# Weights in 1 KB runs, a permuted channel order, a split last unit and a new hand-written order in a two-attention kernel

## The chip, the cores and the metric

The kernel runs on one core of a Trainium2 chip. The metric is the device time of one execution in microseconds. PE is the matmul engine, PEld its weight loads, DVE, ACT and POOL are the three elementwise engines, and SP is the engine that does little but issue DMA transfers. ACT can issue them too.

## The reference

Two attentions follow each other. The second is a layer of four attention experts, of which each row takes the two with the largest gate logits.

```python
# 1: B, H, S, D = 4, 8, 768, 64; n_global, n_local = 8, 96
scores = q @ k.T / sqrt(D) - slope[h] * dist          # dist: row - column, or n_local for a far global key
keep = (column < n_global) | (0 <= row - column < n_local)
x = softmax(where(keep, scores, -1e9)) @ v            # then (B, S, H*D) with H*D = 512 channels

# 2: E = 4 experts, Hd = 64, the two best of four per row
logits = x @ w_gate
for e in range(E):
    ye = causal_softmax((x @ wq[e]) @ (x @ wk[e]).T / sqrt(Hd)) @ (x @ wv[e]) @ wo[e]
    out += weight_of(e, top2(logits)) * ye            # softmax over the two best logits
```

## The kernel before, in words

The rows are cut into 24 units of 128 rows (4 batches of 6; u counts them). Every unit goes through the same stages, and the string `ORDER` says by hand in which order the stages of all units are put into the program: a slot is a stage's two letters, the unit and, where there is a choice, the engine (`a` ACT, `g` POOL, `v` DVE, `s` SP). Each engine works through its own part of that list strictly in order.

- `lk lq lv` load a unit's keys, queries or values (256 KB, in runs of 256 bytes) into one of six buffers for each of the three, on SP's queue or on ACT's (L238). `wi` loads the weights of an expert projection (512 KB; 0 is wk, 1 wq, 2 wv, 3 wo, and 4 the small gate), `wc` turns them into 16 bits.
- `kc qc vc vx` cast keys, queries and the two parts of values to 16 bits (L258, L267). `tk tq` transpose keys and queries on PE, and one copy (L285) brings both to `kqT`.
- `sa sb` make the local scores of a unit, in two halves: first a matmul with the bias table `biasT` (L345), then keys times queries (L352), then one exponential on ACT (L355). `gs vg` do the same for the eight global keys.
- `va vb` multiply scores and values (L381) in one PSUM buffer of two banks, `zps`. DVE takes the reciprocal of the sums (L388) and multiplies (L390), which gives `x`. `tx` transposes x (L402, L403).
- `pk pq pv` project x to the experts' keys, queries and values (L414, L428); `ro` takes a step of the routing (L533 to L557).
- `ca cb cc` make causal scores (L459) and exponentials (L462), `ma` zeroes what lies above the diagonal (L474).
- `za zb` multiply scores and values of the experts (L487) in the same PSUM buffer; DVE normalizes and weighs them after `zb` (L494 to L498), which gives `zs`. `tz` transposes it (L509, L512), `ou` multiplies by wo (L519), copies (L522) and stores (L523).
- `wm` puts in matmuls on the identity that nobody reads, while PE waits at the start (L248).
- `xb` makes the bias table, `xm xc xk xs xi` other constants. `ck` checks that all row sums were in range (L741, L742); their count decides at the very end whether a slow general path has to follow. With these inputs it doesn't.

PSUM has three pools: `psS` with two buffers of two banks (scores), `psZ` with one of two banks (both attentions' values), and `psT` with two buffers of one bank (transposes, projections, outputs).

The projections sum over the 512 channels of x in four groups of 128 (`ko`). Which channels form a group doesn't matter, as long as x and the weights agree. The loads of the weights are written so:

```python
issue(w32s[i][:, :, :, :],
      (moe_wk, moe_wq, moe_wv)[i].rearrange("e (ko kp) d -> kp e ko d", kp=P))
```

Group ko is here made of the channels from 128*ko on, and a partition's row of a weight is four runs of 64 numbers for each expert.

Of the kernel before, what the change touches and what calls it, by code (L numbers as in the profile page):

```python
# [18 lines left out]
P = 128  # L19
# [3 lines left out]
def kernel(  # L23
# [59 lines left out]

    def bias_constants(_):
        V.tensor_copy(rel[:, :], rel_i[:, :])
        ge = const.tile([P, W], F32, name="ge")
        V.tensor_scalar(ge[:, :], rel[:, :], 0.0, None, op0=Alu.is_ge)
        lt = const.tile([P, W], F32, name="lt")
        V.scalar_tensor_tensor(lt[:, :], rel[:, :], float(NL), ge[:, :],
                               op0=Alu.is_lt, op1=Alu.mult)  # L90
        V.tensor_scalar(lt[:, :], lt[:, :], -1.0, -NEG, op0=Alu.add, op1=Alu.mult)
        V.tensor_scalar(rel[KB:P, :], rel[KB:P, :], slopes[1] / slopes[0], None, op0=Alu.mult)
        for p in range(NP):
            V.scalar_tensor_tensor(biasT[:, p, :], rel[:, :], -slopes[2 * p] / sc1, lt[:, :],
                                   op0=Alu.mult, op1=Alu.add)
# [57 lines left out]
    def weights_in(i, on):  # L153

        issue = queues[on]
        if i == 4:
            w32s[i] = wst.tile([P, NK, E], F32, name="wg32", tag="wg32", bufs=1)
            issue(w32s[i][:, :, :], moe_w_gate.rearrange("(ko kp) e -> kp ko e", kp=P))
            return
        w32s[i] = wst.tile([P, E, NK, Hd], F32, name="w32", tag="w32")  # L160
        if i < 3:
            issue(w32s[i][:, :, :, :],
                  (moe_wk, moe_wq, moe_wv)[i].rearrange("e (ko kp) d -> kp e ko d", kp=P))
        else:
            issue(w32s[i][:, :, :, :].rearrange("p e k d -> p (e k d)")
                  .rearrange("p (a m) -> p a m", a=NEP),
                  moe_wo.rearrange("(a b) d m -> (b d) a m", b=2))
# [31 lines left out]
    NC, current = 120, {}  # L199
# [33 lines left out]
    s16s, zs_, x16s, routing, zss, zts, tps, ppss, zs2 = ({} for _ in range(9))  # L233
# [7 lines left out]
    def keep_warm(n):  # L241
# [5 lines left out]
        for _ in range(n):  # L247
            mm(current["z"][:, 0, 4 * P - 2 * NC:4 * P].rearrange("r (a n) -> r a n", a=2),  # L248
               lhsT=ident[:, :], rhs=ident[:, 0:NC].unsqueeze(1).to_broadcast([P, 2, NC]),
# [110 lines left out]
    def global_values(u):  # L360
# [3 lines left out]
        for hf in range(2):  # L364
            r = slice(hf * Dh, hf * Dh + Dh)
            mm(zs_[u][:, hf, 0:HG * VW].rearrange("r (h d) -> r h d", h=HG),  # L366
# [3 lines left out]
    def local_values(u, i):  # L370
# [4 lines left out]
        for hq in (2 * i, 2 * i + 1):  # L375
            for prev in range(2 if ri else 1):
                for c in range(2):
                    for hf in range(2):
                        r = slice(hf * KB, hf * KB + KB)
                        at = c * (2 * P - KB) + prev * P  # L380
                        mm(zs_[u][:, hf, hq * VW:(hq + 1) * VW],  # L381
# [3 lines left out]
        if i == 1:  # L385
            z4 = zs_[u][:, :, 0:HG * VW].rearrange("r a (h d) -> r a h d", h=HG)
            rinv = rinv1[:, b, ri, :].rearrange("r (a h) -> r a h", a=2)
            V.reciprocal(rinv, z4[:, :, :, Dh])  # L388
            x16s[u] = pp.tile([P, 2, HG, Dh], F16, name="x16", bufs=5)
            V.tensor_tensor(x16s[u][:, :, :, :], z4[:, :, :, 0:Dh],  # L390
                            rinv.unsqueeze(3).to_broadcast([P, 2, HG, Dh]), op=Alu.mult)

    def turn_x(u, on):

        xTs[u] = pp.tile([P, NK, P], F16, name="xT", bufs=4)
        x16 = x16s[u][:, :, :, :].rearrange("r a h d -> r (a h d)")
# [80 lines left out]
    def causal_values(u, i):  # L477
# [6 lines left out]
        z_ps = zs2[u][:, 0, 0:E * VW].rearrange("r (e d) -> r e d", e=E)  # L484
        for e in range(i * E // 2, (i + 1) * E // 2):
            for ci in range(n):
                mm(z_ps[:, e, :], lhsT=a2[:, e % 2, (e // 2) * n + ci, :],  # L487
                   rhs=held("v2buf", b * NT + ci)[:, e, :], start=(e == 0 and ci == 0), stop=True,
                   skip_group_check=True)
        if i == 0:  # L490
            return
        assert next(routing[u // NH], "end") == "end"
        rinv = rinv2[:, b, ri, :]
        V.reciprocal(rinv, z_ps[:, :, Hd])  # L494
        ce = pp.tile([P, E], F32, name="ce")
        V.tensor_mul(ce[:, :], rinv, wts[u // NH][:, ri % NH, :])
        zss[u] = pp.tile([P, E, Hd], F16, name="zs")
        V.tensor_tensor(zss[u][:, :, :], z_ps[:, :, 0:Hd],  # L498
                        ce[:, :].unsqueeze(2).to_broadcast([P, E, Hd]), op=Alu.mult)

    def turn_z(u, on):
        zts[u] = pp.tile([P, NEP, P], F16, name="zt")
        if on == "s":
            nc.sync.dma_start_transpose(zts[u][:, :, :],
                                        zss[u][:, :, :].rearrange("r e d -> r (e d)"))
            return
        zt_ps = psT.tile([P, NEP, P], F16, name="ztps", tag="t")
# [6 lines left out]
    def output(u, on):  # L514
        b, ri = divmod(u, NT)
        assert 3 in ready
        o_ps = psT.tile([P, D], F32, name="ops", tag="t")
# [5 lines left out]
        dma(out[b, ri * P:(ri + 1) * P, :], o_sb[:, :])  # L523

# [34 lines left out]
    def general_path(ctx):  # L559
# [35 lines left out]

        ident32 = gc.tile([P, P], F32, name="ident32")
# [20 lines left out]
        with tc.For_i(0, B, 1) as b:  # L617
# [43 lines left out]
            for ri in range(NT):  # L661
                l_ps = gp.tile([P, MAXB], F32, name="gs", tag="s", bufs=2)
                for ko in range(NK):
                    mm(l_ps[:, 0:E], lhsT=xT[:, ko, ri * P:(ri + 1) * P],
                       rhs=wvg16[:, ko, E * Hd:E * Hd + E],
# [6 lines left out]
            for e in range(E):  # L672
                for w, dst, nm in ((wq16, qs, "q"), (wk16, ks, "k")):
                    d = gb.tile([Hd, S], F16, name=f"g{nm}T{e}")
                    for c in range(2):
                        p_ps = gp.tile([P, MAXB], F32, name="gs", tag="s", bufs=2)
                        for ko in range(NK):
                            mm(p_ps[0:Hd, 0:S // 2], lhsT=w[:, ko, e // 2, e % 2, :],
# [6 lines left out]
                for ct in range(NT):  # L685
                    p_ps = gp.tile([P, MAXB], F32, name="gs", tag="s", bufs=2)
                    for ko in range(NK):
                        mm(p_ps[:, 0:Hd], lhsT=xT[:, ko, ct * P:(ct + 1) * P],
                           rhs=wvg16[:, ko, e * Hd:(e + 1) * Hd],
# [55 lines left out]
    def branch_hint(_):  # L745
# [8 lines left out]
        "vs": (select_values,), "xb": (bias_constants,), "xi": (half_identities,),  # L754
# [9 lines left out]
    }  # L764
    for slot in ORDER.split():
        stage, *args = stages[slot[:2]]
        if slot[-1].isalpha():
# [7 lines left out]
    n_f = const.tile([1, 1], F32)  # L775
    V.reduce_sum(n_f[:, :], n_ps[:, :], axis=Ax.X)
    n_i = const.tile([1, 1], I32)
    V.tensor_copy(n_i[:, :], n_f[:, :])
# [13 lines left out]
xb0 lk0s kc0v lq0s az0v az1g lk1s xi0a xs0v xk0g lq1a wm14 tk0 qc0g lv0s kc1g lk2s lq2s lk3a  # L792
wm5 tq0a lq3s xc0g lv1a lv2s lq4s lk4a qc1v lq5s vc0g vx0g wm4 tk1 tq1v xm0v lk5s wm10 sa0 sb0
wm10 vs0 gi0 wi0a wm2 gs0 lk6s kc2v qc2v tk2 tq2v wm3 gs1 lq6s wm7 vg0 kc3g va0 vb0 vc1g vx1v
qc3a sa1 az2g sb1 tk3 tq3v tx0v wi1a vg1 az3g qc4a vc2g kc4g vx2v wm2 va1 wm4 sa2 sb2 vb1 qc5g
gs2 kc5a wc0g tk4 tq4v tx1v az4v lv3s vg2 va2 lv4s vb2 sa3 sb3 tk5 tq5v wm6 tx2v kc6a lq7s wi2a
qc6v wm4 sa4 sa5 tk6 vc3g tq6v pk0 sb4 sb5 wc1v pk1 wm2 gs3 wm2 pq0a vx3v pq1a gi1 vg3 vc4g
vx4g wi4s lv5s va3 vb3 lk7a ca0 ma0 pk2 pq2v tx3v ca1 vg4 va4 vb4 lq8s ca2 pk3 pq3a lk8s vc5v
vx5v cb2 vg5 wc2g lv6s kc7g lq9s pv0v pv1v lq10a lk9s qc7g qc8g kc8g ca3 cb3 tk7 lv7s tq7v pv2v
ro0 va5 sa6 tk8 tq8v tx4v vc6g vx6g lk10a lk11s vb5 sb6 gs4 lv8s ro0 pv3v pk4 qc9g pq4v ro0 ro0  # L800
lq11s lq12a ma1 vs1 lk12s lk13a sa7 tx5v kc9g pv4v kc10g ma2 vg6 va6 ro0 vb6 ca4 tk9 tq9v pk5
lk14s lq13s lv9a pq5v cb4 tx6v sb7 vc7v qc10g qc11a vx7g vc8g tk10 tq10v pv5v kc11g kc12g lq14a
qc12g cc4 vg7 va7 lq15s vb7 ro0 ro0 pk6 pq6a tk11 tq11v vx8g sa8 sb8 tx7v lk15s kc13g kc14g za0
qc13g zb0 lv10a tk12 tq12v gi2 pv6a sa9 sa10 ro1 ro1 lv11s lv12s vc9v vg8 va8 vb8 pk7 pq7a vx9g
tk13 tq13v lk16s lk17s gs5 ca5 qc14g lq16s tz0v za1 lq17s ro1 tk14 tq14v zb1 tx8a ro1 sb9 vc10g
vx10g sb10 kc15a pv7v pv8v vc11g vg9 va9 kc16a vb9 sa11 sa12 tz1v ro1 lq18s kc17v pk8 pq8a za2
ro1 tk15 zb2 sb11 sb12 qc15g tq15v tx9a vc12g vx11g vg10 va10 lk18s vx12g qc16g qc17v vb10 gs6
vs2 tk16 tq16v wi3s qc18g kc18g tk17 tq17v ma3 cb5 vg11 ma4 lk19s va11 lv13s lv14s cc5 tx10v
lv15s tk18 tq18v vb11 ca6 pv9v pv10a ro1 sa13 ro2 sa14 lq19s lq20s gi3 lq21s wc3g za3 ro2 zb3
ou0v ou1a vc13g ro2 ca7 lq22s ca8 vx13g vg12 ma5 va12 vb12 tx11v pk9 pq9v za4 ro2 lk20s kc19g  # L810
zb4 lk21s lk22s lv16s ma6 tz2a ro2 sb13 sa15 tx12v qc19v qc20g pk10 pq10a vc14g vx14g kc20g ma7
tz3v vg13 vc15g ro2 va13 vb13 lv17a cb8 gs7 ma8 ou2v tk19 tq19v lk23s lv18a za5 sb14 sb15 tz4v
zb5 tx13a pv11v sa16 ro2 sb16 vg14 va14 vb14 pk11 ro3 lv19s lv20a pq11a pv12v sa17 za6 zb6 ro3
ro3 vc16g vx15g vx16g ou3a ou4v qc21v ca9 lv21s cb9 tk20 kc21g tq20v za7 pk12 zb7 pq12a tx14v
vc17g ca10 vx17g ro3 cb10 vg15 va15 qc22g tz5v tz6v vb15 ou5a vc18g vc19g tk21 tq21v sa18 vc20v
sb17 kc22g kc23g za8 zb8 tx15a pk13 pq13v ca11 vg16 cc10 va16 pv13v lv22a pv14v cb11 ma9 vb16
gs8 ou6a pk14 pq14v ca12 vx18g vg17 va17 vb17 ca13 tz7v ro3 pk15 ro3 ro3 vx19v pq15a sb18 vs3
tx16v tx17v za9 zb9 ro4 pk16 lq23s pq16a ou7v ro4 lv23s qc23g cc11 vg18 va18 vc21g vb18 pv15a
tk22 tq22v sa19 sa20 ma10 pv16v ma11 za10 tz8a zb10 sb19 sb20 ro4 ro4 ro4 pv17v tz9v ca14 vg19
va19 vb19 ou8a ou9a vx20v sa21 sb21 ro4 ro4 tk23 tq23v ro5 za11 tx18v zb11 tz10a sa22 sb22  # L820
tx19v ma12 pv18v cb14 vg20 va20 vb20 gs9 ro5 ou10a pv19v ma13 vx21g ca15 ca16 vc22g za12 tz11v
zb12 pk17 pq17v pk18 pq18v ro5 ma14 ro5 vc23g cb15 vx22g vg21 va21 vb21 cb16 ro5 tx20v ro5 ro5
pk19 pq19a za13 zb13 pv20a ro6 sa23 sb23 tx21v vg22 va22 vb22 cc16 tz12v pk20 ro6 pq20a za14
# [47 lines left out]
```

## Time and profile before

| | |
|---|---|
| median of 3 runs | 153.25 us (151.09 to 156.71) |
| the profiled execution | 152.97 us |
| its span in the profile | 150.8 us, so 2.2 us lie around it |
| busy share | PE 93%, PEld 73%, DVE 74%, ACT 72%, POOL 60% |
| moved by DMA | 27.77 MB, 85364 packets, of which 82000 under 512 bytes |

The span is what the trace covers, from the first instruction to the last. Busy shares are means over stages that differ: the inputs arrive during the first 87 us, and the last batches are worked off after that. A PE that is shown busy need not be at its peak, since matmuls overlap; the number of matmuls in a stretch says more. The chain that ended last is 74% PE and 11% DMA.

### The profile page before, as it was taken

The numbers are of one execution on the slowest core, as the hardware profiler recorded it, in microseconds if no ns is written. First come the engines' busy times: TensorE is split into PE (matmuls) and PEld (weight loads), VectorE is DVE, ScalarE is ACT, GpSimd is POOL, SyncE is SP. The second block draws the span as 40 slices with busy tenths as digits, with TensorE's granted clock in tenths as the row PEclk, the third lists the DMA queues.
The fourth block names the chain that finished last, engine by engine and source line by source line (L and its number), as shares of the span: only waits on it lengthen the run. The fifth ranks groups of instructions, "written<-read, shape, count | busy, mean of one in ns | idle before, by whom it ended". The sixth has DMA issues, their size and how long they took to land.

```text
span 150.8 us, 7217 instructions
## 1 busy us (share of the span) xinstructions
PE 140.3 (93%) x3029; PEld 110.2 (73%) x3029; DVE 111.4 (74%) x348; ACT 108.1 (72%) x176; POOL 90.2 (60%) x254
## 2 busy tenths in 40 slices
PE   5799999999999999999978999999999999999760
PEld 4567778887778888878757778888778878786520
DVE  4838676687899887878863987687787777778850
ACT  4027657778576888888638998887977978989640
POOL 7278351568878988797827899136286345463200
PEclk9999999999999999999999999999999999999999
DMA  4999998999999989899899963415221005013462
GB/s 99 280 252 286 276 261 192 254 247 238 277 282 275 245 201 249 189 256 208 231 240 288 301 166 113 116 43 142 74 77 70 4 19 195 24 51 127 155 263 97
DMA packets 85364, 27.77 MB, mean 184 GB/s; under 512 B 82000, under 2 KB 82000, under 8 KB 85328
## 3 DMA queue, kind: packets, MB, share of 16 engines
q1 hardware_dynamic: 62496, 21.51, 56.6%
q10 hardware_dynamic: 22832, 5.77, 17.1%
q8 instruction: 24, 0.39, 1.0%
q14 instruction: 12, 0.10, 0.2%
HBM read 20.98 MB, written 6.29 MB: 181 GB/s over the span
## 4 chain that ended last, share of the span: by engine, by line
PE 74%; DMA 11%; DVE 4%; POOL 3%; ACT 2%; issue 1%; SPq 1%; ACTq 0%; POOLq 0%; DVEq 0%
PE pps L414 14%; PE cps L459 7%; PE vps L428 7%; PE tp L283 7%; PE ops L519 6%; PE zps L487 6%; PE zps L381 6%; PE sps L345 5%; PE zps L248 4%; DMA kf<-in_k_dram 4%; DMA vf<-in_v_dram 4%; PE xps L402 3%; PE sps L352 3%; DMA qf<-in_q_dram 3%; PE zps L366 2%; PE ztps L509 2%
## 5 line engine op out<-in xcount | busy, mean ns | idle before, releaser
L462 ACT ACTIVATE a<-cps 128x1024 f16<-128x1024 f32 (+1 forms) x48 | 42.2, 917 | 8.3 <-PE cps L459 6.6
L355 ACT ACTIVATE abuf<-sps 128x636 f16<-128x636 f32 (+1 forms) x48 | 30.6, 686 | 12.8 <-PE sps L352 10.1
L267 POOL CAST vbuf<-vf 64x256 f16<-64x256 f32 x76 | 31.0, 408 | 8.4 <-DMA vf<-in_v_dram 5.2
L474 POOL TENSOR_SCALAR_AFFINE_SELECT a<-a 128x256 f16<-128x256 f16 x48 | 18.3, 409 | 5.1 <-ACT a L462 4.8
L285 DVE COPY kqT<-tp 128x1024 f16<-128x1024 f16 x23 | 15.7, 688 | 6.6 <-PE tp L283 6.1
L390 DVE TENSOR_TENSOR x<-zps,rinv 128x512 f16<-128x512 f32 x24 | 16.6, 691 | 0.8
L487 PE MATMUL zps<-v2buf,a 128*128 128x65 f16 x336 | 16.0, 193 | 0.6 <-DVE zs L498 0.5
L345 PE MATMUL sps<-biasT,ident 64*64 64x318 f16 (+1 forms) x192 | 14.5, 305 | 1.4 <-ACT abuf L355 1.3
L381 PE MATMUL zps<-vbuf,abuf 64*128 64x65 f16 x704 | 15.5, 189 | 0.0
L258 POOL CAST s16k<-kf 128x512 f16<-128x512 f32 x17 | 10.3, 612 | 8.7 <-DMA kf<-in_k_dram 8.3
L487 PEld LDWEIGHTS <-a 128*128 128x128 f16 x336 | 13.3, 97 | 2.1 <-DVE zs L498 0.9
L381 PEld LDWEIGHTS <-abuf 64*128 64x128 f16 x704 | 14.0, 94 | 1.1 <-issue 0.2
L414 PE MATMUL pps<-xT,wk 128*128 128x128 f16 x192 | 14.7, 219 | 0.0
L414 PE MATMUL pps<-xT,wq 128*128 128x128 f16 x192 | 14.5, 219 | 0.0
L248 PE MATMUL zps<-ident 128*128 128x240 f16 x75 | 12.8, 316 | 1.7 <-POOL ident masks.py:199 1.6
L428 PE MATMUL vps<-wvg,xT 128*128 128x260 f16 x96 | 13.9, 275 | 0.0
L459 PEld LDWEIGHTS <-kq 64*128 64x128 f16 x336 | 9.7, 94 | 5.8 <-issue 4.4
L459 PE MATMUL cps<-kq,kq 64*128 64x128 f16 x240 | 13.8, 218 | 0.0
L519 PE MATMUL ops<-wo,zt 128*128 128x512 f16 x48 | 13.5, 380 | 0.4 <-DVE zt L512 0.4
L352 PE MATMUL sps<-kqT 64*64 64x159 f16 (+2 forms) x384 | 13.8, 223 | 0.0
L258 POOL CAST s16q<-qf 128x512 f16<-128x512 f32 x15 | 9.4, 630 | 5.1 <-DMA qf<-in_q_dram 4.9
L414 PEld LDWEIGHTS <-wk 128*128 128x128 f16 x192 | 11.5, 98 | 0.8
(113 smaller groups left out, 286.4 us busy)
## 6 DMA issues: line engine op xcount, KB each, us to landing
out_dram<-osb SPq DMA_DIRECT2D x24, 256.0 KB, 2.3
qf<-in_q_dram SPq DMA_DIRECT2D x20, 256.0 KB, 5.6
kf<-in_k_dram SPq DMA_DIRECT2D x19, 256.0 KB, 5.7
vf<-in_v_dram SPq DMA_DIRECT2D x17, 256.0 KB, 5.5
vf<-in_v_dram ACTq DMA_DIRECT2D x7, 256.0 KB, 4.7
kf<-in_k_dram ACTq DMA_DIRECT2D x5, 256.0 KB, 4.9
qf<-in_q_dram ACTq DMA_DIRECT2D x4, 256.0 KB, 4.5
w<-in_moe_wk_dram ACTq DMA_DIRECT2D x1, 512.0 KB, 5.3
```

Source lines behind the costliest of these rows:

```text
L248: mm(current["z"][:, 0, 4 * P - 2 * NC:4 * P].rearrange("r (a n) -> r a n", a=2), lhsT=ident[:, :], rhs=ident[:, 0:NC].unsqueeze(1).to_bro ...
L258: copies[on](s16s[nm, u][:, :, :], fs[nm, u][:, :, :])
L267: copies[on](o[hf * KB:(hf + 1) * KB, c, :, 0:Dh], fs["v", u][c * KB:(c + 1) * KB, hf * HG:(hf + 1) * HG, :])
L345: mm(s_ps[o, hh, 0:2 * w].rearrange("r (c n) -> r c n", c=2), lhsT=ident2[r, :], rhs=biasT[r, p, 0:w].unsqueeze(1).to_broadcast([KB, 2, w] ...
L355: S_.activation(as_[u][:, :, g, :].rearrange("r h (c n) -> r h c n", c=2)[:, :, :, 0:w], s_ps[:, :, 0:2 * w].rearrange("r h (c n) -> r h c ...
L381: mm(zs_[u][:, hf, hq * VW:(hq + 1) * VW], lhsT=as_[u - prev][r, hq % 2, hq // 2, at:at + P], rhs=held("vbuf", u - prev)[r, c, hq, :], sta ...
L414: mm(p_ps[:, i, ep, :], lhsT=w[:, ko, ep, :, :].rearrange("r a d -> r (a d)"), rhs=xT[:, ko, :], start=(i == 0 and ep == 0 and ko == 0), s ...
L428: mm(v_ps[:, :], lhsT=xT[:, ko, :], rhs=wvg16[:, ko, :], start=(ko == 0), stop=(ko == NK - 1))
L459: mm(s_ps[:, e2, i, :], lhsT=kqs[b * NT + ci][r, 0, ep, :], rhs=kqs[u][r, 1, ep, :], start=(i == 0), stop=True, skip_group_check=True)
L462: S_.activation(a2[:, :, 4 * c:4 * c + len(part), :], s_ps[:, :, 0:len(part), :], func=Exp, scale=sc2)
L487: mm(z_ps[:, e, :], lhsT=a2[:, e % 2, (e // 2) * n + ci, :], rhs=held("v2buf", b * NT + ci)[:, e, :], start=(e == 0 and ci == 0), stop=Tru ...
L519: mm(o_ps[:, :], lhsT=zts[u][:, ep, :], rhs=wo16[:, ep, :], start=(ep == 0), stop=(ep == NEP - 1))
```

## The change

1. The weights wk, wq and wv come in runs of 1 KB: a partition gets four neighbouring channels of an expert (256 numbers). So group ko is now made of every fourth channel, and x is written in that order. The heads stand 128 apart in PSUM instead of 65, so that one access pattern covers all eight. The matmuls that keep PE busy write to the free columns between them.
2. The constants for the bias table are made in two slots, `xb` and `xp`. The masks `xm`, `xc` and the half identities `xi` are made on POOL.
3. The last unit is normalized, transposed and multiplied by wo in halves: experts 0 and 1, then 2 and 3, each half in its own bank. Its output is copied in two halves by DVE and ACT and stored over both queues. Outputs of units 21 and 22 and the transpose of 22 use `psS` instead of `psT`.
4. At the end the sum of the checks is written as a whole number at once.
5. `ORDER` is new throughout. It starts with query tile 0, and 60 matmuls of `wm` are left of 75. ACT issues 7 loads instead of 19. The general path loads its own weights in the old order.

```diff
-            issue(w32s[i][:, :, :, :],
-                  (moe_wk, moe_wq, moe_wv)[i].rearrange("e (ko kp) d -> kp e ko d", kp=P))
+            issue(w32s[i][:, :, :, :].rearrange("p e k d -> p e (k d)"),
+                  (moe_wk, moe_wq, moe_wv)[i].rearrange("e (kp ko) d -> kp e (ko d)", ko=NK))
...
-    NC, current = 120, {}
+    NC, current = 60, {}
...
-                        mm(zs_[u][:, hf, hq * VW:(hq + 1) * VW],
+                        mm(zs_[u][:, hf, hq * P:hq * P + VW],
...
-            x16s[u] = pp.tile([P, 2, HG, Dh], F16, name="x16", bufs=5)
-            V.tensor_tensor(x16s[u][:, :, :, :], z4[:, :, :, 0:Dh],
-                            rinv.unsqueeze(3).to_broadcast([P, 2, HG, Dh]), op=Alu.mult)
+            x16s[u] = pp.tile([P, NK, H, Dh // NK], F16, name="x16", bufs=5)
+            V.tensor_tensor(x16s[u][:, :, :, :].rearrange("r k h d -> r h k d"),
+                            z8[:, :, 0:Dh].rearrange("r h (d k) -> r h k d", k=NK),
+                            rinv.unsqueeze(2).unsqueeze(3).to_broadcast([P, H, NK, Dh // NK]),
+                            op=Alu.mult)
...
+        last = u == NU - 1
+        nz = E // 2 if last else E
...
-        if i == 0:
+        if i == 0 and not last:
             return
...
+    def end_tile(u, first, shape, dtype, name):
+        if u < first:
+            return psT.tile(shape, dtype, name=name, tag="t")
+        return psS.tile(shape, dtype, name=name, tag="s")
...
+    def last_output(ep):
+        b, ri = divmod(NU - 1, NT)
+        if ep == 0:
+            outs["last"] = [psS.tile([P, 2, D], F32, name="ops1", tag="s")] * 2
+        for i in range(2):
+            c = slice(i * D // 2, (i + 1) * D // 2)
+            o_ps = outs["last"][i][:, i, 0:D // 2]
+            mm(o_ps, lhsT=zts[ep, "last"][:, :], rhs=wo16[:, ep, c], start=(ep == 0),
+               stop=(ep == NEP - 1), skip_group_check=True)
+        if ep == 0:
+            return
+        for i, (copy, queue) in enumerate(((V.tensor_copy, dma), (S_.copy, S_.dma_start))):
+            c = slice(i * D // 2, (i + 1) * D // 2)
+            o_sb = pp.tile([P, D // 2], F32, name=f"osb{i}", bufs=1)
+            copy(o_sb[:, :], outs["last"][i][:, i, 0:D // 2])
+            queue(out[b, ri * P:(ri + 1) * P, c], o_sb[:, :])
...
-xb0 lk0s kc0v lq0s az0v az1g lk1s xi0a xs0v xk0g lq1a wm14 tk0 qc0g lv0s kc1g lk2s lq2s lk3a
+bh0 lq0s xm0g xk0g lk0s lk1a xc0g xb0 lq1s lv0s xp0 xi0g lk2s lk3s xs0g qc0v kc0a qc1v kc1a
+wm18 tk0 lq2a az0v lq3a wm7 tk1 kc2g tq0v wm2 tq1a wm13 sa0 wm2 tk2 lk4s gi0 az1g az2g vc0v
...
-ck0 ck1 ca23 bh0 cb23 za21 tz19v zb21 ou18v cc23 tz20v ma22 za22 zb22 tz21a ou19a ou20v ma23 za23 tz22v
-zb23 ou21a ou22a tz23v ou23a ck2
+cb23 ou17v tz19a za21 zb21 cc23 ck0 ck1 ma22 ou18v za22 tz20v zb22 ma23 tz21a ou19a ou20a za23
+tz22a zb23 ou21a ou22a tz23v ty23v ck2 ou23 oy23
```

## The prediction

> **What bounds the kernel now.** I read the page first, then a table of stages, then the waits of the worst stage with the chain that runs through it, then the timeline of the end. The page:
>
> ```profile
> span 150.8 us, 7217 instructions
> ...
> PE 140.3 (93%) x3029; PEld 110.2 (73%) x3029; DVE 111.4 (74%) x348; ACT 108.1 (72%) x176; POOL 90.2 (60%) x254
> ...
> DMA  4999998999999989899899963415221005013462
> ```
>
> The DMA row is full until slice 23 (87 us): inputs flow that long. Stages (columns: stretch, its length, busy us and count of each engine):
>
> ```profile
> 0.00:25.00 25.00, 21.73 (x342) 16.31 (x346) 16.95 (x50) 11.71 (x21) 13.48 (x46) 1.00 1.08 240
> 25.00:75.00 50.00, 50.00 (x1202) 40.63 (x1195) 40.61 (x116) 38.68 (x64) 39.74 (x99) 1.00 1.06 240
> 75.00:80.00 5.00, 3.62 (x79) 2.90 (x78) 2.96 (x9) 2.38 (x5) 1.32 (x4) 1.00 1.06 240
> 80.00:135.00 55.00, 54.95 (x1273) 44.48 (x1272) 41.65 (x137) 46.80 (x75) 32.95 (x98) 1.00 0.39 111
> 135.00:140.00 5.00, 4.93 (x84) 3.00 (x79) 4.47 (x19) 4.80 (x7) 1.96 (x8) 1.00 0.33 121
> 140.00:147.00 7.00, 5.07 (x64) 2.83 (x63) 4.77 (x21) 3.75 (x7) 0.77 (x2) 1.00 0.53 204
> ```
>
> PE sets the pace: 24 matmuls/us from 25 to 75 us, 23 from 80 to 135. It loses time in three places: the start, 75 to 80 us (16/us: 79 matmuls are 3.3 us of work, so 1.7 us lost), and the end. The waits from 60 to 80 us and the chain there name the middle loss:
>
> ```profile
> POOL s16k L258 <- DMA kf<-in_k_dram: 3.8, 2, 3.5
> ACT abuf L355 <- PE vps L428: 2.3, 1, 2.3
> ...
> PE sps L345 <- ACT abuf L355: 1.3, 1, 1.3
> ```
>
> and in the chain, with start and length in us:
>
> ```profile
> 73.47 4.66 DMA qf<-in_q_dram
> ...
> 78.20 0.39 ACTq L238
> ```
>
> ACT was not waiting for PE: its sequencer stood before a load of v (slot `lv18a`) that could not be issued until an earlier q load had landed at 78.13, and the exponential behind it started 2.3 us late. The end:
>
> ```profile
> 143.75 1.02 PE L519 MATMUL ops<-wo,zt 128*128 128x512 f16 x4
> ...
> 144.22 0.42 DVE L498 TENSOR_TENSOR zs<-zps,ce 128x256 f16<-128x256 f32 x1
> ...
> 145.02 0.27 PE L509 MATMUL ztps<-ident,zs 128*128 128x128 f16 x2 [0.24 <-ACT osb L522]
> ...
> 145.33 0.29 DVE L512 COPY zt<-ztps 128x256 f16<-128x256 f16 x1 [0.68 <-PE ztps L509]
> ...
> 145.68 0.60 PE L519 MATMUL ops<-wo,zt 128*128 128x512 f16 x2 [0.39 <-DVE zt L512]
> ...
> 146.32 0.59 ACT L522 COPY osb<-ops 128x512 f32<-128x512 f32 x1 [0.86 <-PE ops L519]
> ```
>
> Last scores times values done at 143.75; then a single file of steps, PE nearly idle, to 146.91; the store and the closing waits take 3.9 us more.
>
> **What the Trainium skill says.** "DMA: Bandwidth & Descriptors", Why small descriptors are slow: each packet has a fixed cost, 27% of a 256-byte one. The trace agrees in direction. ACT's ring moved 22832 packets, 5.77 MB, in 17.1% of 16 engines' span: 0.171 x 150.8 x 16 / 22832 = 18 ns per 256 bytes. SP's ring (62496 packets, 56.6%) holds 3328 of 2 KB; the other 59168 at 18 ns leave 89 ns for each of those, 45 ns per KB instead of 72. Same page, Anatomy of one DMA: the engines that move data don't wait on semaphores, the issuing sequencer does. That is the 2.3 us above. "VectorE: DVE Perf Modes", Mode 1x: the base mode makes no assumptions on strides or PSUM operands. No run of before shows a strided read of this size.
>
> **The change, part by part** (against the profiled execution: 152.97 us, span 150.8; the median shown is 153.25).
>
> 1. *Weights in 1 KB runs.* Three loads of 512 KB: 6144 packets x 18 ns become 1536 x 45 to 72 ns. Saved: 0 to 42 us of engine time, over 16 engines 0 to 2.6 us of supply, all before 35 us. I take 1.2; it pays only where supply binds, so it is joined to part 4.
> 2. *Every fourth channel side by side.* The order of channels on both sides of the projections is the same permutation; matmul shapes and counts stay (heads at a pitch of 128 in the two PSUM banks instead of 65). The multiply that writes x reads PSUM 4 words apart and writes runs of 16. Before: 691 ns for 512 elements, and 424 for 256, so 1.04 ns an element, one per cycle. At that rate a stride has nothing to spoil: I take 0; below zero there is no reason; above, half rate is 24 x 0.53 us, kept for a rival.
> 3. *First loads, bias constants in two parts, masks moved to POOL.* Before, the first scores start at 11.03, behind key tile 1, third on SP's ring (landed just before POOL's cast at 8.05). Now key tile 1 has ACT's first slot, and query tile 1 takes the third place on SP: cast by 8.5, transposed by 8.85, then ACT's copy (1.01, as kqT by ACT before) under 13 warm-ups (1.3 us): scores at 10.2. DVE has 0.27+1.10+0.32+0.24+0.26 of constants, 4 small ones of 0.15 and 1.03 of biases first, about 5.9, then the query casts: not late. So 0.8 us earlier. But the stage after it is fed by DMA at an unchanged rate: counting slots, k12's cast has 41 tile volumes ahead in both orders, and as much PE work done. I take 0; bounds -0.8 and +0.3. Fifteen warm-ups fewer (75 to 60, 0.1 us each) stood in waiting time: 0.
> 4. *The new order, middle.* Loads on ACT's queue go from 19 to 7, and after the first 30 us only one (`lq23a`) is left. The 1.7 us that PE lost go, about 12 x 0.4 us of issuing leave ACT, and SP has them instead; they use the same engines. The first outputs now stand behind lk22 instead of ahead of lk20. What is late next: v14's cast (65 tile volumes ahead, one less through part 1), which POOL takes in order ahead of v13's second half and a mask. Before, the count of landed volumes ran at 1.04 us each up to 53 and 1.10 up to 66. At 1.05 v14 lands at 71, about when PE comes there; at 1.10 at 74, 3 us late. With part 1, I take -2.0; bounds -3.5 and +1.5. Casts and copies by engine come out even: by the row durations DVE 59.7 to 59.0 us, ACT 29.0 to 30.1, POOL 55.3 to 54.5.
> 5. *The checks of row sums* (`ck0 ck1`, 1.0 us of DVE at 138.9) stood ahead of unit 21's normalization, and unit 22's matmuls waited 0.7 us for it (PEld L487, from 140.26). They now come after it: -0.6; bounds -0.8 and 0.
> 6. *Last unit in halves.* T = 143.75. Half 0's normalization runs under half 1's 12 matmuls (0.36) and the outputs of 21 and 22 (4 x 0.217). Half 1: 0.17 + 0.16 + (0.157 + 128 x 1.04 ns = 0.29) and gaps: T+0.76. PE is free at T+0.87 and no longer waits for ACT's copy (other PSUM pool); two transposes and their latency T+1.15, two small copies (0.2 each, half of the 0.286 row and a fixed part) T+1.5, four matmuls of 256 columns, the last two after it, T+1.85; copies of 256 columns on DVE (0.43, as v2buf's cast) and ACT (0.37) together T+2.3. Before: T+3.16. So -0.85, with the store unchanged (2.3 us to landing; two halves on two rings can save 0.1). `ck2` (0.43 of DVE) lies under the four matmuls. I take -0.9; bounds -1.2 and -0.5. One conversion fewer at the very end (0.14) is under the store.
>
> Sum: -2.0 -0.6 -0.9 = -3.5: 149.4 us (span 147.3).
>
> **Rivals.**
> - *Supply takes the place of ACT's wait.* PE reaches v13's and v14's values early and waits behind POOL's cast. For: POOL's waits above, 3.5 us for one key tile; two thirds of the former ACT loads now stand in SP's single file. Against: SP's own order puts no output ahead of them. The -2.0 becomes 0 to +0.5: 151.5 to 152. 0.27.
> - *The strided multiply runs at half rate.* x takes 1.2 us instead of 0.69, between the one PSUM buffer of attention and the projections, 24 times. For: never seen here. Against: one element per cycle already. It decides from about 1.0 us up; if 60% of 12.7 us reaches PE's path: 149.4 + 7.6 = 157, slower. 0.09, with a somewhat smaller share for a milder form, 154.
> - *A denser plan than the sum shows.* The whole order is new; if the start's 0.8 us keeps and PE runs at 24 a us throughout (1273 + 84 + 64 matmuls after 80 us: 59 us instead of 67, of which a quarter is got): 149.4 - 0.8 - 2 = 146.6. 0.16.
> - *The new order is worse in places that I can't see*: 153.5. 0.06.
>
> **How the numbers follow.** Forecast 0.42: 149.4, own range 147.8 to 151. Range 146.3 to 152.9, which takes in the denser plan's value and the supply rival. A measurement of this kernel tells about 2% from no change; 2% below 153 is 150.0. Faster: the denser plan and nearly four fifths of the forecast, 0.16 + 0.33 = 0.49. Slower: the strided multiply and part of the worse order, 0.13. The rest, 0.38, same.
>
> **What would show it.** Right: no idle of 1 us or more on ACT ahead of an exponential from 70 to 80 us; the gap of PE there gone; x at 0.69 us; the last store issued about 2.3 us after the last scores times values; the first scores before 10.5 us. Wrong: POOL waiting for v14 with PE idle at 70 to 78 us; x above 0.8 us; fewer than 23 matmuls per us after 80 us.

## The result, and the profile after

The changed kernel is slower: 172.91 us median (171.84 to 174.87), beside 153.39 us for the kernel before in the same runs. The ratio is 1.134 (95% interval 1.112 to 1.156), where the prediction had 149.4 us; ratios, here and below, leave out executions in which the core ran disturbed. Its profiled execution took 171.84 us with a span of 170.0. The page of the kernel after, with the rows of total busy time, DMA share, rate and DMA queues:

```profile
span 170.0 us, 7194 instructions
...
PE 140.9 (83%) x3016; PEld 110.7 (65%) x3016; DVE 109.8 (65%) x335; ACT 109.7 (64%) x181; POOL 93.5 (55%) x266
...
DMA  5999899999896999988979949013210413322450
GB/s 116 218 218 221 177 313 239 196 212 224 176 226 146 230 200 213 224 185 185 254 168 212 260 140 227 13 64 125 83 48 4 129 66 125 125 94 99 185 197 2
...
q1 hardware_dynamic: 73952, 25.57, 64.9%
q10 hardware_dynamic: 6528, 1.71, 5.2%
```

And the rate row of the kernel before:

```profile
GB/s 99 280 252 286 276 261 192 254 247 238 277 282 275 245 201 249 189 256 208 231 240 288 301 166 113 116 43 142 74 77 70 4 19 195 24 51 127 155 263 97
```

PE's busy time is unchanged (140.9 against 140.3 us, at a granted clock of 0.97 against 1.00); all of the 19 us is waiting. The DMA row is as full of nines as before, and that is what misled: a full row says that the engines had packets in hand, not how fast these went. The rate row says it: in the first slices that carry nothing but loads, 218, 218, 221 GB/s in place of 280, 252, 286. The same 16 engines, no more bytes, and about a fifth slower. The stages of the kernel after:

```profile
0.00:25.00 25.00, 19.09 (x325) 14.21 (x329) 14.73 (x42) 11.11 (x18) 14.78 (x52) 0.95 1.07 209
25.00:75.00 50.00, 41.09 (x961) 33.17 (x954) 31.41 (x83) 31.03 (x54) 31.61 (x78) 0.99 0.99 206
75.00:80.00 5.00, 2.58 (x72) 1.97 (x69) 2.76 (x7) 3.73 (x6) 0.95 (x2) 1.00 0.87 190
80.00:135.00 55.00, 52.63 (x1187) 42.73 (x1191) 40.07 (x126) 40.83 (x67) 35.40 (x103) 0.97 0.55 135
135.00:140.00 5.00, 5.00 (x135) 3.95 (x124) 3.60 (x13) 4.68 (x8) 3.77 (x13) 1.00 0.24 74
140.00:163.00 23.00, 20.40 (x366) 14.66 (x364) 17.06 (x66) 18.00 (x30) 7.02 (x23) 1.00 0.33 126
```

From 25 to 75 us the last column falls from 240 to 206 GB/s and PE's matmuls from 1202 to 961. The waits of the kernel after from 70 to 81 us, where the prediction looked for ACT's wait and its successor:

```profile
POOL s16k L264 <- DMA kf<-in_k_dram: 4.7, 2, 3.7
...
PE tp L289 <- POOL s16k L264: 3.2, 1, 3.2
```

ACT's wait is gone; a key tile is late instead, POOL waits for it and PE for POOL. Three single lines answer other steps: the multiply with the strided read of PSUM, the first local scores, and the last store of ACT's half:

```profile
L397 DVE TENSOR_TENSOR x<-zps,rinv 128x512 f16<-128x512 f32 x24 | 16.6, 691 | 0.8
...
10.74 0.33 PE L351 MATMUL sps<-biasT,ident 64*64 64x318 f16 x4
...
163.30 0.37 ACTq L566 DMA_DIRECT2D out_dram<-osb  x1
```

**What slows the loads** is, as the experiments show, two things that the diff hardly shows. First, the change drops a constant of four bytes, `n_f` (the count was first summed as a float and then turned into a whole number; now it is summed as one). It was the last tile but one of the pool of constants and took 32 bytes of every partition. All buffers that are allocated later lie 32 bytes lower in the built program: the input buffers begin at 78304 in place of 78336. 78336 is 306 times 256; 78304 is 32 bytes short of that. The buffers are 2 KB each and follow each other, so every run of 256 bytes that a load of keys, queries or values writes now lies across a multiple of 256. Second, the new order leaves ACT 7 loads of 19: 73952 of the packets are now in one ring (q1) and 6528 in the other (q10), against 62496 and 22832.

### The profile page after: what moved, and what is told of

It reads as the page before. It is cut to its first block, busy times and chain, and to the rows that moved or that the text cites. A ratio compares the mean times of both kernels' runs of the same rounds, so it can differ in the third digit from the quotient of the medians.

```text
span 170.0 us, 7194 instructions
## 1 busy us (share of the span) xinstructions
PE 140.9 (83%) x3016; PEld 110.7 (65%) x3016; DVE 109.8 (65%) x335; ACT 109.7 (64%) x181; POOL 93.5 (55%) x266
## 3 DMA queue, kind: packets, MB, share of 16 engines
q1 hardware_dynamic: 73952, 25.57, 64.9%
q10 hardware_dynamic: 6528, 1.71, 5.2%
## 4 chain that ended last, share of the span: by engine, by line
PE 40%; DMA 26%; SPq 14%; POOL 7%; DVE 4%; issue 2%; ACT 2%; POOLq 0%; DVEq 0%
SPq L244 13%; DMA kf<-in_k_dram 13%; PE pps L423 6%; DMA qf<-in_q_dram 6%; PE ops L534 5%; PE cps L468 5%; PE zps L498 5%; DMA vf<-in_v_dram 4%; PE vps L437 4%; DMA w<-in_moe_wk_dram 3%; PE zps L387 3%; PE tp L289 2%; PE sps L351 2%; PE xps L411 2%; PE ztps L524 2%
## 5 line engine op out<-in xcount | busy, mean ns | idle before, releaser
L273 POOL CAST vbuf<-vf 64x256 f16<-64x256 f32 x74 | 29.8, 403 | 8.0 <-DMA vf<-in_v_dram 4.9
L264 POOL CAST s16k<-kf 128x512 f16<-128x512 f32 x15 | 9.2, 611 | 19.8 <-DMA kf<-in_k_dram 18.3
L289 PE MATMUL tp<-ident,s16k 128*128 128x128 f16 x96 | 9.6, 224 | 9.7 <-POOL s16k L264 6.2
L423 PE MATMUL pps<-xT,wq 128*128 128x128 f16 x192 | 15.1, 223 | 0.2 <-POOL wq L180 0.2
L498 PEld LDWEIGHTS <-a 128*128 128x128 f16 x336 | 13.4, 98 | 2.5 <-DVE zs L511 1.1
L428 ACT CAST kq<-pps 128x512 f16<-128x512 f32 x13 | 7.5, 586 | 10.3 <-PE pps L423 10.1
L289 PEld LDWEIGHTS <-s16k 128*128 128x128 f16 x96 | 6.0, 99 | 12.2 <-POOL s16k L264 6.9
L468 PE MATMUL cps<-kq,kq 64*128 64x128 f16 x240 | 13.1, 218 | 0.3 <-DVE kq L428 0.3
L264 POOL CAST s16q<-qf 128x512 f16<-128x512 f32 x17 | 10.3, 611 | 5.1 <-DMA qf<-in_q_dram 4.5
```

Source lines behind the costliest of these rows:

```text
L264: copies[on](s16s[nm, u][:, :, :], fs[nm, u][:, :, :])
L273: copies[on](o[hf * KB:(hf + 1) * KB, c, :, 0:Dh], fs["v", u][c * KB:(c + 1) * KB, hf * HG:(hf + 1) * HG, :])
L289: nc.tensor.transpose(tps[u][:, i, p, :], s16[:, p * P:(p + 1) * P], ident[:, :])
L423: mm(p_ps[:, i, ep, :], lhsT=w[:, ko, ep, :, :].rearrange("r a d -> r (a d)"), rhs=xT[:, ko, :], start=(i == 0 and ep == 0 and ko == 0), s ...
L468: mm(s_ps[:, e2, i, :], lhsT=kqs[b * NT + ci][r, 0, ep, :], rhs=kqs[u][r, 1, ep, :], start=(i == 0), stop=True, skip_group_check=True)
L498: mm(z4[:, e // nz, e % nz, :], lhsT=a2[:, e % 2, (e // 2) * n + ci, :], rhs=held("v2buf", b * NT + ci)[:, e, :], start=(e % nz == 0 and c ...
```

## The experiments

Ratios are to the kernel before, run beside each; the interval is 95%.

**One ring, in the kernel before** (`e1_before_one_ring`): all 19 loads of ACT are put on SP's queue, each at its place in the order.

```diff
-lk0s kc0v lq0s ... xk0g lq1a wm14 ... lq2s lk3a
+lk0s kc0v lq0s ... xk0g lq1s wm14 ... lq2s lk3s
```

> The kernel before with one thing changed: all its loads are issued by SP, at the same places of the order (19 of them were ACT's). Theory A (one issuer's ring alone moves inputs more slowly than two together: 1.1 us against 0.91 us for a 256 KB tile in the two traces): the inputs end some 10 us later, 160 to 167 us, tile landings 1.05 to 1.15 us apart, under 230 GB/s. Theory B (rings don't matter, loads on ACT only hold ACT up): 150 to 153 us, ACT's 2.3 us idle at 76 us is gone. Theory C (the new order asks for tiles in a worse sequence; queues don't matter): 152 to 154 us.

1.086 (1.078 to 1.095). The kernel before, its code and buffers untouched, loses 8.6% when SP issues everything. My theory that a load on ACT's queue only costs ACT time falls with this run: with the second ring the inputs come faster.

**Two rings, in the kernel after** (`e2_after_two_rings`): every third tile load on ACT, 25 in all.

> The changed kernel with one thing changed: every third tile load goes to ACT's queue, at its place in the order (25 tile loads on ACT instead of 6; the weights stay on SP). Theory A: landings back at 0.9 to 1.0 us per tile up to 80 us, 156 to 164 us. Theory B: more loads on ACT hold it up more, 174 to 178 us. Theory C (sequence of tiles): 171 to 174 us.

1.134 (1.126 to 1.142): nothing comes back. So the one ring can't be all.

**The changed code with the old order** (`e3_after_code_old_order`), and the same with the loads of v17 and v18 on SP and the first two checks behind unit 21's normalization (`e4_mix`; the expectation counts v16 too, which SP issued already):

```diff
-zb23 ou21a ou22a tz23v ou23a ck2
+zb23 ou21a ou22a tz23v ty23v ck2 ou23 oy23
```

> The code of the changed kernel (1 KB weight runs, permuted channels, split last unit, late outputs in the scores' PSUM pool) with the order of the kernel before, its queues too; only the last slots and the second half of the bias constants are adapted. If order and queues alone made it slow (A or C): 150.5 to 153 us, the tail 0.9 us shorter. If the code did (strided multiply, weights in 1 KB runs): 160 us or more.

> As the one with the new code and the old order, with the loads of v16, v17 and v18 issued by SP instead of ACT, and the first two checks of row sums put behind unit 21's normalization. Theory A: these loads come late, when the inputs are nearly all in, so one ring costs little and ACT's 1.3 and 2.3 us before them go: 1 to 2.5 us less than the old order with the new code, 148 to 151 us. If the waits on ACT were only covering a later limit (v landing on POOL): no difference.

1.071 (1.068 to 1.074) and 1.067 (1.059 to 1.075). With 19 loads on ACT and the order of before (e3), the new code alone is 7% slower, although none of its instructions takes longer. Its first loads, issued at the same times as before's, landed later from the first ones on (the third at 6.68 us, not 6.20; the sixth at 10.31, not 8.89). That pointed away from order and waits, to where the bytes go.

**Only the address, in the kernel before** (`e8_before_shifted`): the constant of four bytes is taken from another pool, which lies after the buffers. Instructions and order are identical; the buffers start at 78304.

```diff
-    n_f = const.tile([1, 1], F32)
+    n_f = pp.tile([1, 1], F32, name="n_f", bufs=1)
```

> The kernel before, instruction for instruction, with the 4-byte tile n_f moved to another pool, so that everything allocated after the constants starts 32 bytes lower (input buffers at 78304). D: 158 to 164 us, the first eight tiles land by 11.5 us instead of 9.9. If addresses don't matter: 150 to 153 us.

1.085 (1.076 to 1.095). The rate row of this kernel's page, beside before's 280, 252, 286, 276:

```profile
GB/s 116 223 218 218 222 218 195 213 213 187 219 231 222 220 219 197 222 170 258 222 222 209 220 244 228 70 127 68 130 93 47 64 4 65 138 64 64 133 251 145
```

**The address repaired, in the changed code**: one constant of 32 bytes more, so that the buffers start at 78336 again. `e7_old_order_padded` is e3 with it, `e5_after_padded` is the kernel after with it, `e6_after_padded_two_rings` is e2 with it.

```diff
+    pad = const.tile([1, 8], F32, name="pad")
+    V.memset(pad[:, :], 0.0)
     n_i = const.tile([1, 1], I32)
```

> The code of the changed kernel with the order and queues of the kernel before, with the 32 bytes. D: 149 to 151.5 us, at or a little under the kernel before, of which 0.9 us is the tail. If the 1 KB runs or the permuted channels cost the 7%: 160 us still.

> The changed kernel with one small tile more among the constants (32 bytes a partition, one memset), so that the input buffers start 32 bytes higher in a partition, at 78336 as in the kernel before, instead of 78304. Theory D (256-byte packets into rows that are not aligned to 64 bytes or more cap the input DMA near 220 GB/s, whatever the rings) with A (one ring alone caps it near 220 too): the changed kernel still has one ring, so only part comes back: 160 to 168 us. D without A: 147 to 152 us. A without D: 172 to 174 us.

> The changed kernel with the 32 bytes and with every third tile load on ACT's queue. D with A: both caps are gone, landings 0.90 to 0.95 us apart where the queues are full, 147 to 153 us. D or A alone: 157 us or more. If the new sequence of tiles or ACT's holding up (B, C) carries much of the loss: 160 us or more.

e7: 0.9996 (0.995 to 1.004), where e3 had 1.071: 32 bytes are worth the whole loss of the new code. e5: four runs between 163.5 and 170.1 us beside 152.4 for before, too far apart for a ratio. The kernel after is still far behind with the address repaired. e6: 1.061 (1.051 to 1.072), where e2, with the same loads on ACT, had gained nothing; its runs lie at 160.9 to 164.6 us, under e5's, though not by much. What is left in e6 is partly of my making: a load of v that I put on ACT landed at 22.4 us, and POOL waited 7.7 us for it.

**Both faults in the kernel before** (`e11_before_one_ring_shifted`: e8 with e1's order), and **both repaired in the kernel after** (`e10_after_padded_early_act`: the pad, and 16 more loads on ACT, those that stand 32 slots or more ahead of their casts, 22 in all):

> The kernel before with both faults: every load on SP, and the buffers 32 bytes lower. Alone they cost 8.6% and 8.5%. If each is a cap of its own near 220 GB/s, together they cost little more than one, 9 to 12%: 164 to 170 us. If they add: 175 to 180 us.

> The changed kernel with the 32 bytes, and 22 loads on ACT, the added 16 chosen among those that stand at least 32 slots ahead of their cast (in the earlier two-ring version a v load on ACT landed 7.7 us after POOL had begun to wait for it). If that choice made the two-ring version slow: 150 to 156 us. If the new sequence, whose loads stand nearer to their casts than before, is itself the cost: 158 to 164 us.

1.115 (1.108 to 1.122) and 1.024 (1.019 to 1.030). The two faults don't add, as if each were a cap on the same rate; together, in the order of before, they cost 11.5%, beside the 13.4% of the kernel after. With both repaired, the new order is 2.4% slower than before: that is what is left for the order and for what my choice of loads did to it. The stretch from 35 to 75 us in one table, from the tables of stages:

| kernel | GB/s | PE matmuls | ratio |
|---|---|---|---|
| before | 244 | 968 | 1 |
| e7, new code, old order, address repaired | 242 | 961 | 0.9996 |
| e1, before, one ring | 226 | 803 | 1.086 |
| e8, before, address shifted | 214 | 814 | 1.085 |
| e11, before, both | 204 | 702 | 1.115 |
| after | 202 | 799 | 1.134 |
| e10, after, both repaired | 248 | 934 | 1.024 |

One thing stays open here. In the trace of e5 (address repaired, 6 tile loads on ACT, one execution, and the longest of its four) this stretch moved only 205 GB/s, less than e1's 226 with a single ring. If that is typical, the new order on nearly one ring is held back by more than the ring's own rate; which of its loads wait, and for what, no run isolated.

**The loads by themselves** (`e12_loads_only`): ten groups of 14 tiles of 256 KB each, with one or two rings, at offsets of 0, 32, 64 or 128 bytes from a multiple of 256, in runs of 256 bytes or 2 KB.

> Loads alone, no attention (the output is zeros): ten stages of 14 tiles of 256 KB, with runs of 256 bytes or 2 KB, over SP alone or SP and ACT in turn, to buffers that start on a multiple of 512 bytes or 32, 64 or 128 bytes past one. D with A: two rings, aligned, 256-byte runs 0.90 to 0.95 us a tile; 32 bytes past 1.10 to 1.20; one ring 1.05 to 1.15 aligned and 1.10 to 1.20 not. 64 and 128 past: like aligned if lines of 64 bytes count, like 32 past if the 256 or 512 do. Runs of 2 KB: 0.7 to 0.9 us everywhere, less sensitive. If neither matters: all stages of one run length alike.

The table of stretches, one inside each group, in the order: two rings with 0, 32, 64 and 128 bytes, one ring with 0 and 32 (all in runs of 256 bytes), then two rings with 0 and 32 and one ring with 0 and 32 in runs of 2 KB. The columns are stretch, length, busy time of DVE and POOL, PE's clock, DMA share, GB/s:

```profile
5.00:13.00 8.00, 1.37 (x9) 0.00 (x0) 1.00 1.28 288
18.00:31.00 13.00, 1.69 (x11) 0.00 (x0) 1.00 1.39 218
35.00:48.00 13.00, 1.70 (x11) 0.00 (x0) 1.00 1.38 218
52.00:65.00 13.00, 1.69 (x11) 0.00 (x0) 1.00 1.35 218
69.00:79.00 10.00, 1.39 (x9) 0.00 (x0) 1.00 1.08 245
84.00:91.00 7.00, 0.89 (x6) 0.00 (x0) 1.00 1.33 221
101.00:106.00 5.00, 1.05 (x8) 0.00 (x0) 1.00 1.05 406
110.00:116.00 6.00, 1.38 (x9) 0.00 (x0) 1.00 1.05 389
120.00:125.00 5.00, 1.23 (x8) 0.00 (x0) 1.00 1.05 406
129.00:134.00 5.00, 1.08 (x7) 0.00 (x0) 1.00 1.05 388
```

This is one execution, but the differences between the groups are large, and they fit the kernels. Runs of 256 bytes that start on a multiple of 256 go at 288 GB/s over two rings and 245 over one. Off it they go at 218 over two rings, whether by 32, 64 or 128 bytes, and at 221 over one. That is why e2 gained nothing. Runs of 2 KB lose 4% and need no second ring.

The share column (time that packets took, as a share of 16 engines, where packets overlap) is higher in the slow groups than in the fast one: 1.39 against 1.28. Share is not throughput. But share and rate together give the mean time of one packet, 16 x 256 bytes x share / rate, and there the two faults differ. On the multiple a packet takes 18 ns, with two rings and with one alike (1.28 and 288, 1.08 and 245); 32 bytes off it takes 26 and 25 ns. In the kernel too: e8's ACT ring moved its 22832 packets in 19.9% of 16 engines' span of 163.7 us, 22.8 ns each, where the prediction worked out 18 for before. So a wrong address makes packets slower, by 7 to 8 ns on the mean. A single ring doesn't; it leaves the engines without packets at times. In the trace eight of the 13 gaps between the landings of the aligned one-ring group are 0.90 to 0.95 us, as with two rings, and four are 1.24 to 1.71. SP was issuing nearly all that time, most issues taking 0.74 to 0.90 us; for a tile in runs of 2 KB an issue took 0.33 us. That the time of issuing is what leaves the engines short is likely from this, but no run changed it alone.

**What became of the steps that the loads hid.** The next runs start from e7 or from before, so both faults are out of them.

`e9_mix_padded` is e4 with the pad: the loads of v17 and v18 moved to SP, and the checks `ck0 ck1` behind unit 21's normalization, where the changed kernel has them.

> The code of the changed kernel, the order of the kernel before with the loads of v16 to v18 issued by SP and the first two checks behind unit 21's normalization, and the 32 bytes. If the steps of the prediction that had nothing to do with addresses and rings hold (ACT's wait at 76 us 1.7 us, the checks 0.6 us, the tail 0.9 us, the weights up to 1.2 us): 147.5 to 150 us, 1 to 3% under the kernel before. If those waits are only handed to something else: 150.5 to 152.

1.013 (1.008 to 1.018): against e7 no gain, rather a loss, from the two together. The run doesn't tell them apart.

`e13_split_last` gives the halves of the last output two PSUM tiles. In e7, as in the kernel after, ACT's copy of its half began only when DVE's copy of the other had ended (146.36 us, after 0.80 us of waiting for DVE), because both read parts of one tile.

```diff
-            outs["last"] = [psS.tile([P, 2, D], F32, name="ops1", tag="s")] * 2
+            outs["last"] = [psS.tile([P, D // 2], F32, name="ops1", tag="s"),
+                            psT.tile([P, D // 2], F32, name="ops2", tag="t")]
```

> e7 (the changed code with the order of before and the padded constants) with the two halves of the last output in two PSUM tiles in place of one. If ScalarE's copy of its half waits for VectorE's copy because both read one tile, ScalarE starts its copy together with VectorE's, the last store is issued about 0.4 us earlier than in e7 (2.3 us after the last scores-times-values instead of 2.70), and the time is 0.3 to 0.4 us lower: ratio to before 0.997. If the wait has another cause (PSUM bank, the matmuls' own order), the copies stay one after the other and nothing moves.

The two copies run together, and from the start of the last reciprocal to the last store's issue it is 143.73 to 145.98 = 2.25 us, not 2.70. The time doesn't show it: 1.005 (1.002 to 1.008), on another chip than e7's. The lines of e13 show another wait ahead of it. PE, from 141.58 us on:

```profile
141.58 0.52 PE L498 MATMUL zps<-v2buf,a 128*128 128x65 f16 x12
...
143.17 0.52 PE L498 MATMUL zps<-v2buf,a 128*128 128x65 f16 x12 [0.96 <-DVE zs L511]
```

The second half's 12 matmuls wait 0.96 us for DVE's normalization of the first half. Before had no such wait; its 24 matmuls ran through. DVE meanwhile is in a single file, from the chain of e13 (start, length, what):

```profile
137.09 0.68 DVE osb L537
137.77 0.18 DVE low L799
...
138.48 0.24 DVE low L800 x2
138.72 0.20 DVE zt L527
```

Three runs asked what paces this end. `e15_split_last_late_act_off` moves three late copies from ACT to DVE (`ou16 tz21 pq23`, from `a` to `v`), on the theory that ACT, 93% busy from 130 to 140 us, sets the pace:

> e13 with three late copies moved from ScalarE to VectorE (the output of unit 16, the transposed z of unit 21, a projection pair of 23; 1.5 us of ScalarE from 128 to 142 us). If ScalarE paces the last 15 us, the end comes up to 1 us earlier than e13. If it does not, or VectorE (88% busy from 135 to 140 us) is as full, no change or up to +0.5 us.

1.014 (1.007 to 1.020), slower than e13: the theory falls. DVE has no 1.5 us to spare there. `e18_last_unit_apart` is e13 with the last unit's second half of values in a PSUM tile of its own:

```diff
+        if last and i == 1:
+            z4[1] = psT.tile([P, nz * VW], F32, name="zps3", tag="t")[:, :].rearrange(
+                "r (e d) -> r e d", e=nz)
```

> e13 with the second half of the last unit's scores times values in a PSUM tile of its own. In e13 TensorE waits 0.96 us (142.2 to 143.17) before that half's 12 matmuls, for VectorE's normalization of the first half, which reads the one PSUM tile of both halves; in before the 24 matmuls run through. If that shared tile is where the lead of 1.2 us is lost, the wait goes, the last store is issued 0.5 to 0.9 us earlier after the start of the last unit's matmuls than in e13, and the time is 0.5 to 0.9 us below e13 (ratio to before 0.999 against 1.005). If VectorE, which has copies and the normalization in one file there, is what holds the end, the wait only changes its place and the time stays within 0.2 us of e13.

0.998 (0.996 to 1.001), against e13's 1.005 on another chip, and the wait is gone:

```profile
141.83 0.52 PE L501 MATMUL zps<-v2buf,a 128*128 128x65 f16 x12
...
142.30 0.53 PE L501 MATMUL zps<-v2buf,a 128*128 128x65 f16 x12
...
145.66 0.37 ACTq L570 DMA_DIRECT2D out_dram<-osb  x1
```

Both halves had lain in different PSUM banks all along; what the program waited for was the tile. `e19_last_unit_apart_checks_in_gaps` is e18 with the two checks moved ahead of DVE's file, into two stretches in which it waits for PE, and `e17_before_checks_in_gaps` is the kernel before with that move alone:

```diff
-ck0 ck1 ca23 bh0
+ca23 bh0
...
-pq23a ro7 za19
+pq23a ro7 ck0 za19
...
-ou14a pv21v cb20
+ou14a pv21v ck1 cb20
```

> e18 with the two checks of row sums (1.0 us of VectorE) moved out of VectorE's file, which runs from 133.7 to 141.4 us without a gap, into two gaps ahead of it (0.56 and 0.70 us, where it waits for TensorE). If VectorE's file paces the last 15 us, 0.6 to 1.0 us below e18 (ratio 0.993). If PE's own work paces it, nothing.

> The kernel before with only the same move of the two checks into VectorE's gaps at about 131 and 134 us. If VectorE's file paces the end of before too, -0.6 to -1.0 us: ratio 0.994 to 0.996. My prediction had -0.6 for taking them out from ahead of unit 21's normalization; the changed kernel and e9 only put them two units later in the same file. If nothing moves, the step was wrong altogether.

0.9966 (0.994 to 0.999) and 0.997 (0.994 to 1.000). In e19 the last store is issued at 144.67 us in place of e18's 145.66, with the same 24 units behind it; the medians move less, 150.48 against 150.88. Each ratio alone is hard to tell from its base, but both go the same way. e19 is the fastest of the versions with the changed code, 0.3% under the kernel before; but the kernel before with that one move is as fast, 150.40 us beside 150.48.

The trace of e17 shows something more. Its program is that of before up to the two checks at 131 and 134 us, and still the loss of PE at 75 to 80 us, the largest that the prediction priced, isn't there. Its stage, in the columns of the table of stages, and then ACT's lines:

```profile
75.00:80.00 5.00, 5.00 (x140) 4.30 (x139) 3.59 (x11) 3.50 (x6) 3.27 (x9) 1.00 1.12 253
...
75.47 0.41 ACTq L238 DMA_DIRECT2D vf<-in_v_dram  x1
76.46 1.29 ACT L355 ACTIVATE abuf<-sps 128x636 f16<-128x636 f32 x2 [1.02 <-PE sps L352]
```

PE does 140 matmuls there, not 79. The load `lv18a` goes out at 75.47 us, not 78.20, and ACT waits 1.02 us before the exponential, not 2.30. Until 76 us the two traces have the same 1560 matmuls; but in the execution of before that was profiled (152.97 us) the loads had fallen behind, 221 GB/s from 60 to 65 us where e17 (150.15 us) has 261. The wait belonged to that execution; the kernel before doesn't always have it.

`e14_split_last_weights_aligned` puts the weights' buffer, which lies 64 bytes short of a multiple of 256 in before, on one as well (on top of e13):

> e13 with the staging buffer of the weights also on a multiple of 256 bytes (34048 in place of 33984; the inputs' buffers stay on one, 78592). If alignment is worth for 1 KB runs what it is for 2 KB runs in the loads alone[...], three loads of 512 KB save 0.1 to 0.4 us each of supply before 35 us; supply has slack later, so the time moves by 0 to -0.5 us against e13. If it counts as for 256-byte runs (27%), -0.5 to -1 us.

1.008 (1.005 to 1.011), e13 1.005 (1.002 to 1.008): no gain. Three loads of 512 KB in runs of 1 KB are too little, or long enough runs, to matter. The run shows one thing besides. In e12 the aligned buffers start on multiples of 512 bytes; here the input buffers start at 78592, 307 times 256, and from 25 to 75 us they fill at 247 GB/s, e13's at 246. So a multiple of 256 is enough.

## Why the prediction was wrong

The sign was wrong. The range missed by 20 us, and the cause stood in none of the rivals. (The sum itself slips a little: 152.97 less 3.5 is 149.5, not 149.4.)

- *The step that failed first* is the edit that I costed at "one conversion fewer at the very end (0.14)". As an instruction that is right. The tile that goes with it moved every input buffer by 32 bytes, and I didn't look at addresses. Alone it makes before 8.5% slower (e8).
- *The step that failed second* is in part 4: the loads moved from ACT's queue to SP's "use the same engines", at no cost. The Trainium skill says the same ("DMA: Bandwidth & Descriptors", Issuing engines are not separate DMA queues, and Rules for kernel authors: spreading DMAs over several issuing engines doesn't help bandwidth, it only saves the sequencer's time of issuing, which is usually small). For runs of 256 bytes this case measured otherwise, 288 GB/s over two rings and 245 over one, and 8.6% in the kernel (e1); nor is the time of issuing small here, some 0.8 us of SP for a tile that lands every 0.9. The measurement decides. For runs of 2 KB the page is right (406 and 406). The profile of before held the hint: its rate row has slices of 280 to 301 GB/s, above the 245 that e12 shows for one ring and above every slice of e1 (at most 275).
- *"The stage after it is fed by DMA at an unchanged rate"* (part 3), and the counts of landed volumes at 1.04 to 1.10 us each in part 4, rest on both. After's tiles landed at 1.19 us each, on the mean, from 34 to 42 us. The rival on supply had the place right (POOL behind a late tile, though of keys and not v14, and PE behind POOL, at 70 to 78 us) and the size wrong, +0.5 us at most, because it counted tiles in line and not the time of each.
- *Weights in runs of 1 KB* (-1.2 us of supply): e7 moved 266 GB/s from 10 to 35 us, before 249, which is 0.43 MB or some 1.7 us of supply more; the other profiles of the repaired code in the old order have 255 to 266, and e17, with before's code, 249. That is in line with the step, for these first 35 us. From 25 to 75 us nothing is left of it (243 to 248, before 240, e17 249), and e7's time shows no gain. No run isolated it.
- *ACT's wait at 76 us* (-2.0 with part 1), the largest term of the sum, was read rightly from the trace but priced as if every execution had it. In e17, the same program up to 131 us, it is absent, and in e7, with before's order and its loads on ACT, too (142 matmuls from 75 to 80 us, not 79). So no moved load was needed to remove it, and there was little to gain: the 152.97 us from which I subtracted held the wait, while before's median in the later runs is 150.9 to 152.4 us. A lead of e7 or e13 over the profiled before after 80 us is this wait and not a gain of theirs: at 100 us e7 has done 2095 matmuls, before 2083, e17 2116.
- *Tail in halves* (-0.9): the part counted from T, the last values, was -0.42 in e7 (2.70 us from the last reciprocal to the last store, 3.12 before) because of the shared output tile, and with that mended -0.87 in e13 (2.25) and -0.95 in e18 (143.49 to 145.66 = 2.17). But T itself moved, which the step left out: from the start of the last unit's first 12 matmuls to the last store it is 4.18 us before, 4.86 in e7, 4.40 in e13, 3.83 in e18. As built in e7, halving the last unit cost 0.7 us; with both tiles apart it saves about 0.35. My line "half 0's normalization runs under half 1's 12 matmuls" was false for one PSUM tile.
- *The checks* (-0.6): behind unit 21's normalization, in the same file, they gave no gain that e9 shows (which moves two loads too). Out of the file they give perhaps 0.3%, 0.4 us (e17; e19 against e18), at the edge of what the runs can tell.
- *First loads replanned* (first scores at 10.2): 10.74, before 11.03, at the slower rate. What that was worth later no run isolated.
- *The strided multiply*: 691 ns, to the nanosecond as before, as "VectorE: DVE Perf Modes" of the Trainium skill (Mode 1x) let one expect. That rival is out.

So the code of the change, rid of the two faults and of two shared tiles, is worth nothing that these runs can tell from zero: e18 has 0.998 (0.996 to 1.001), and e19's 0.997 is what before's own code reaches with the same move of the checks (e17). I had -3.5 us. What the new order would give with loads well spread over two rings stays open: e10 is one such spread, chosen by rule, and it is 2.4% slower than before.

## What to carry to other kernels

When a diff adds or removes any tile, even of four bytes, compare the addresses of the buffers that DMAs write in short runs, and pin them to a multiple of 256 bytes. Read supply from the GB/s row, not from a full DMA row, and before moving loads to one queue, ask whether slices of that row lie above what one ring reaches. Before pricing a wait, look whether a second execution has it. When work is split in halves to overlap, give each half its own tile, or the halves wait for each other.

## What the runs showed of the hardware that was not expected

- Runs of 256 bytes written into SBUF off a multiple of 256 bytes: 218 GB/s instead of 288 (two rings), the same at 32, 64 and 128 bytes off. "DMA: Bandwidth & Descriptors" of the Trainium skill (How a descriptor splits into AXI transactions) tells that a descriptor that doesn't start on 256 bytes pays extra beats when reading. By an estimate from that page, if writes counted as its reads do, a run of 256 bytes at 32, 64 and 128 past would cost 9, 10 and 12 beats instead of 8; the writes measured here took a third longer (288/218 = 1.32) at all three. Runs of 2 KB lost 4% (406 to 389).
- One ring reaches 245 GB/s with runs of 256 bytes, two reach 288, with packets of 18 ns in both: what is lost lies between the packets. With runs of 2 KB both reach 406.
- Off the multiple, a second ring adds nothing (218 with two, 221 with one).
